# Buffers, tiles and evicting engine in the third stage of a convolution that runs before a recurrent attention loop

## The chip, the cores and the metric

The kernel runs on one core of one Trainium2 chip. The metric is the device time of one execution in microseconds (us). A core has five engines with an in-order instruction stream each: TensorE (PE; its weight loads are shown as PEld), VectorE (DVE), ScalarE (ACT), GpSimd (POOL) and SyncE (SP). DMA transfers are issued from the streams of SP, ACT and POOL, and 16 DMA engines carry them.

## The reference

Two independent parts are computed from separate inputs and laid side by side in the output (2048 rows; 1024 columns each).

Part A is a long convolution with gating:

```
k_shift = sum over t of k_pad[:, t:t+S, :] * shift_k[:, 3-t]     # 4 taps
kv      = k_shift * v
y       = irfft(rfft(kv, 2S) * rfft(ssm_k, 2S))[:S] + kv * ssm_D
a       = q * y
```

Part B is attention with a recurrent memory: the 2048 rows of x are cut into 64 segments of 32 rows, and for each segment in turn

```
h = concat(mem (8 rows), x_s (32 rows))
q, k, v = h @ Wq, h @ Wk, h @ Wv                # 32 heads of 128
o = softmax(mask(q k^T * scale)) v @ Wo
mem, out_s = o[:8], o[8:]
```

## The kernel before

**The order of the work.** `run_a` computes part A (function `a_kernel`), and what part B needs and does not depend on the memory is woven into it: `a_kernel` calls `fill()` once per step of its stages 2 and 3, and `fill` (L663) adds one piece of part B's preparation to the program. After that come the remaining pieces, the V pass, and then the loop over 64 segments, which takes most of the time.

**Part A in three stages.** The transforms are matrix products. Stage 1 (L242) writes the transformed rows of kv and of the kernel to DRAM (`SU1`, `SK1`). Stage 2 (L301 to L398, 17 sets of two halves, so 34 calls of `fill`) reads them back, multiplies and writes `SZ` to DRAM (L318 to L323); its TensorE order is fixed by hand (`tc.manual_schedule`, L384). Stage 3 (L400 to L421) has 16 steps t. Each loads a tile `zt` from `SZ` (L407, 512 KB), runs four matmuls against `G2h` into a PSUM tile `pt` (L410; shown as `y_ps`), and multiplies it with the query on VectorE into `ot` (L417). Every second step loads a query tile `qt` (L414, 512 KB) for two steps and stores an `ot` tile for two steps through POOL (L419, 512 KB). There are four `zt`, two `qt` and two `ot` buffers and three PSUM tiles of two banks.

**The pieces of part B.** `dense` (L617) makes 16 units for one weight group: eight matmuls into a PSUM tile (L623, `kb_ps`), then `evac` (L610) copies it to the `stage` tile. Three groups follow each other, (0,1), (1,0) and (1,1), 48 units. `fill` adds a unit in every call of stage 3 and in two of three calls of stage 2, so that units 22 to 31 end group (1,0) in the last part of stage 2 and in stage 3, units 32 to 38 of group (1,1) lie in stage 3, and nine more come after it (L741). After the 16th unit the group's four stores `RKQ<-stage` are issued from ACT. The last three weight tiles of group (1,1) are loaded by SP (L573 and L577, `pw<-in_B_Wq_dram`, 512 KB each) into places that the last unit of group (1,0) gives free. `x_load` (L588) loads two blocks of x for use by `x_block` (L594): eight transposes into a PSUM tile (L601, `xt_ps`), two VectorE copies into `xt` (L604, L605), one store `REC<-xt` through POOL (L606, 256 KB). Five of the 16 blocks, 11 to 15, fall into stage 3. `kb_ps` and `xt_ps` share two PSUM tiles.

```
def evac(dst, src):
    if units[0] < STAGE3:              # 34: the calls of fill in stage 2
        nc.scalar.copy(dst, src)
    else:
        nc.vector.tensor_copy(dst, src)
```

So ScalarE evicts the units of stage 2 but for the very last one, VectorE those of stage 3, the nine behind it and the V pass. The X tiles and `xt` tiles are the single buffers `wring2` and `wring3`, which the loop's weight ring uses later.

**After stage 3.** SP loads a tile `part` (L869), then the 16 tiles of Wv (L573 and L577; `Wres`, `Wmore`, `pw`), most of them into memory that part A's tiles had. The V pass (L755 to L768) is 32 units of eight matmuls (L764, `vb_ps`), evicted by VectorE and stored by ACT. Then the segment loop begins (L925).

**What sets the order.** Outside the parts ordered by hand, a scheduler places the instructions of each engine, and each engine runs them in that order. A buffer that is used again makes the next writer wait for the last reader. Each transfer signals one of eight completion counters for those issued from SP and ACT together, and one of eight for POOL's, in turn; a transfer waits until the one eight places earlier on its counter has landed. So up to eight transfers from SP and ACT are under way at once, and one instruction that waits in SP's stream holds back all later loads.

Of the kernel before, what the change touches and what calls it, by code (L numbers as in the profile page):

```python
# [9 lines left out]
BF = mybir.dt.bfloat16  # L10
# [23 lines left out]
STAGE3 = 34  # L34
# [18 lines left out]
def a_kernel(ctx: ExitStack, tc, q, k, v, shift_k, ssm_k, ssm_D, outa, ps_sum, slot4, slot16, stage1_done, fill):  # L53
# [19 lines left out]
    def pair_rows(ap2d, t):  # L73
        return ap2d.rearrange("(p r) d -> p (r d)", r=16)[:, 1024 * t:1024 * t + 2048]

    with ExitStack() as c1:
        cw = c1.enter_context(tc.tile_pool(name="a_cw", bufs=1, side="right"))
        io = c1.enter_context(tc.tile_pool(name="a1_io", bufs=2, side="right"))
        wk = c1.enter_context(tc.tile_pool(name="a1_wk", bufs=3, side="right"))
# [221 lines left out]
    with ExitStack() as c2:  # L301
        gio = c2.enter_context(tc.tile_pool(name="a2_io", bufs=3, side="right"))
        wk = c2.enter_context(tc.tile_pool(name="a2_wk", bufs=3, side="right"))
# [95 lines left out]

    with ExitStack() as c3:  # L400
        io = c3.enter_context(tc.tile_pool(name="a3_io", bufs=4, side="right"))
        wk = c3.enter_context(tc.tile_pool(name="a3_wk", bufs=3, side="right"))
        ps_big = c3.enter_context(tc.tile_pool(name="a3_ps", bufs=3, space=PSUM))
        for t in range(16):
            pt = ps_big.tile([128, 1024], F32, tag="big", name="y_ps")
            zt = io.tile([128, 2, 1024], BF, tag="zt", name="zt")
            nc.sync.dma_start(zt[:], SZ.rearrange("m (r h) d -> r m h d", h=2)[t])  # L407
            for hf in range(2):
                for h in range(2):
                    nc.tensor.matmul(pt[:, hf * 512:(hf + 1) * 512], lhsT=G2h[h][:, :],  # L410
                                     rhs=zt[:, h, hf * 512:(hf + 1) * 512], start=(h == 0), stop=(h == 1))
            if t % 2 == 0:
                qt = io.tile([128, 2048], BF, tag="qt", bufs=2, name="qt")
                nc.sync.dma_start(qt[:], pair_rows(q, t))  # L414
                ot = wk.tile([128, 2048], BF, tag="ot", bufs=2, name="ot")
            half = slice(1024 * (t % 2), 1024 * (t % 2) + 1024)
            nc.vector.tensor_tensor(out=ot[:, half], in0=pt[:], in1=qt[:, half], op=ALU.mult)  # L417
            if t % 2:
                nc.gpsimd.dma_start(outa.rearrange("(p r) d -> p r d", r=16)[:, t - 1:t + 1, :],  # L419
                                    ot[:].rearrange("p (r d) -> p r d", r=2))  # L420
            fill()  # L421


def b_kernel(ctx: ExitStack, tc, x, mem0, Wq, Wk, Wv, Wo, outb, n_seg, run_a):
# [28 lines left out]
    def dram_chunk(ch):  # L453
        m, a, g = ch
        return Wo_v[a] if m == 3 else W_v[m][a, g]

    def dst_view(ap, ch):
        return ap.rearrange("p (hh d) -> p hh d", hh=2) if ch[0] == 3 else ap

    def stream_src(ch):  # L460
        return WS[ring_order.index(ch), :, 0:2048]
# [19 lines left out]
    base = ctx.enter_context(tc.tile_pool(name="b0_base", bufs=1, side="right", reuse_waits="tile"))  # L481
# [8 lines left out]
    def pair():  # L490
        turns["pair"] ^= 1
        return base.tile([128, 2048], BF, tag=f"wring{2 + turns['pair']}", name="pair")

    def slot16(shape, dt, name):
        turns["stage"] ^= 1
        return base.tile(shape, dt, tag=f"stage{turns['stage']}", name=name)
# [3 lines left out]
    def pw(k=None):  # L500
        if k is None:
            k = pw_next[0] % 8
            pw_next[0] += 1
        return pring.tile([128, 2048], BF, tag=f"pw{k}", name="pw")
# [80 lines left out]
    copies = []  # L585
    loaded = {}

    def x_load(b):  # L588
        t = base.tile([128, 2048], BF, tag="wring2", name="X_sb")
        x_loads.append(nc.sync.dma_start(t[:].rearrange("p (b d) -> p b d", b=2),  # L590
                                         x[b * 128:(b + 2) * 128, :].rearrange("(b p) d -> p b d", b=2)))
        loaded[b], loaded[b + 1] = t[:, 0:1024], t[:, 1024:2048]

    def x_block(b):  # L594
        X_sb = loaded.pop(b)
        if b % 2 == 0:
            t = base.tile([128, 2048], BF, tag="wring3", name="xt")
            xts[b], xts[b + 1] = t[:, 0:1024], t[:, 1024:2048]
        tp = ps0.tile([128, 1024], BF, tag="ps0", name="xt_ps")
        for kc in range(8):  # L600
            nc.tensor.transpose(tp[:, kc * 128:(kc + 1) * 128], X_sb[:, kc * 128:(kc + 1) * 128], ident[:])  # L601
        xt = xts.pop(b).rearrange("p (s k t) -> p s k t", s=4, k=8)
        rows = tp[:].rearrange("p (k j t) -> p j k t", k=8, j=4)
        nc.vector.tensor_copy(xt[:, :, :, NM:SEG], rows[:, :, :, 0:NX])  # L604
        nc.vector.tensor_copy(xt[:, :, :, 0:NM], rows[:, :, :, NX:SEG])  # L605
        rec_stores.append(nc.gpsimd.dma_start(REC[:, 4 * b:4 * b + 4, :], xt.rearrange("p s k t -> p s (k t)")))  # L606
# [1 line left out]
    xts = {}  # L608
    rec_stores, x_loads = [], []
    def evac(dst, src):  # L610
        if units[0] < STAGE3:
            nc.scalar.copy(dst, src)
        else:
            nc.vector.tensor_copy(dst, src)
# [35 lines left out]
    def store():  # L650
        if stores:
            nc.scalar.dma_start(*stores.pop(0))

    units = [0]
    blocks = list(range(n_seg // 4))
    wo_copies = [ch for ch in ring_order if ch[0] == 3 and ch not in (KEPT_A, KEPT_B)]

    def q1_load(kc, k, ins):
        res[1, kc, 1] = pw(k)[:]
        with tc.issue_after(ins):  # L660
            group(1, 1, which=[kc], ws=q1, held=True)

    def fill(behind=None):  # L663
        store()
        n = units[0]
        units[0] += 1
        if n == 0:
            x_load(0)
        if n >= WO_COPY and wo_copies:
            ch = wo_copies.pop(0)  # L670
            with tc.issue_after(rec_stores[-1].ins):
                nc.gpsimd.dma_start(dst_view(stream_src(ch), ch), dram_chunk(ch))
        if n in Q_LOAD:
            i = Q_LOAD.index(n)
            q1_load(kept_q1[i][1], 4 + i, behind.ins)
        if n > 5 and n % 2 and copies:
            with tc.issue_after(rec_stores[-1].ins):
                copied.append(nc.gpsimd.dma_start(*copies.pop(0)))
        if n % 3 == 2 and blocks:
            b = blocks.pop(0)  # L680
            x_block(b)
            if b % 2 and blocks:
                x_load(b + 1)
        if n >= STAGE3 or n % 3 != 2:
            next(rest, None)

# [6 lines left out]
    def more(i):  # L693
        return wres3.tile([128, 2048], BF, tag=f"Wmore{i}", name="Wmore")
# [43 lines left out]
    with c0p:  # L738
        temps = dict(zip(v_temp, homes_v))
        wv = [group(2, 0, temps), None]  # L740
        for _ in rest:  # L741
            store()
        wv[1] = group(2, 1, temps)
        for i, ch in enumerate(v_temp):
            if i >= 2:
                home = (lambda i=i: more(i)) if i < len(v_temp) - 2 else (lambda k=i - len(v_temp) + 4: pw(k))
                at_hand[ch] = (wv[ch[2]][ch[1]], home)
        while stores:
            store()
        with tc.issue_after(got[-1].ins):  # L750
            for _ in range(2):
                fetch()
        n_k = len(own[0, 0])
        late = late[n_k:-2] + late[4:n_k] + late[:4] + late[-2:]
        for g in range(2):  # L755
            ws = wv[g]
            if g == 0:
                vsts = slot16([128, 4, 4, 512], BF, "vst")
            for tb in range(4):
                vst = vsts[:, tb] if g == 0 else pair()[:].rearrange("p (c w) -> p c w", c=4)  # L760
                for c in range(4):
                    ps = ps0.tile([128, 512], F32, tag="ps0", name="vb_ps")
                    for kc in range(8):
                        v_last = nc.tensor.matmul(ps[:], lhsT=xbt(kc)[:, 16 * tb:16 * tb + 16, :].rearrange("p s t -> p (s t)"),  # L764
                                                  rhs=ws[kc][:, c * 512:(c + 1) * 512], start=(kc == 0), stop=(kc == 7))
                    evac(vst[:, c, :], ps[:])
                nc.scalar.dma_start(
                    VBD[g, 16 * tb:16 * tb + 16].rearrange("s t h e -> (s t) (h e)"), vst.rearrange("p c w -> p (c w)"))  # L768
            if g == 0:
                with tc.issue_after(got[-1].ins):  # L770
                    place_late(4, stage_home)
                    for i in [*range(len(v_temp) - 2, n_more), *range(len(v_temp) - 2)]:
                        place_late(1, lambda: more(i))
                    place_late(1, lambda: pw(2))
                    place_late(4, stage_home)
        assert len(late) == len(at_hand) + 1
# [441 lines left out]
```

## Time and profile before

| | us |
|---|---|
| median of 3 runs | 1750.67 |
| lowest and highest run | 1744.69, 1751.97 |
| the profiled execution | 1745.92 |
| its span in the profile (1.8 lies around it) | 1744.1 |
| last instruction of stage 2's scatter lands; first `zt` load issued | 265.5 |
| last `ot` of stage 3 ends | 329.5 |
| V pass, first PSUM tile complete | 348.2 |
| V pass ends | about 403 |

| engine | busy us | share of the span |
|---|---|---|
| PE | 1645.4 | 94% |
| DVE | 1057.9 | 61% |
| ACT | 665.0 | 38% |
| POOL | 348.9 | 20% |

Times inside the profile are counted from the span's start. A line of the timeline gives start, duration, engine, source line, operation, tile written `<-` tiles read, form and count, and in brackets how long the engine had stood still before it and what released it. An engine name with a q (SPq, ACTq) is its stream issuing a transfer. A line of the stage table gives the stretch, its length, the busy time and the number of instructions of PE, PEld, DVE, ACT and POOL, the TensorE clock granted (1.00 is full), the DMA engines' busy share (it can pass 1 a little) and the GB/s moved. A line of the chain gives start, duration and what the end of the program was waiting for in that piece.

### The profile page before, as it was taken

How to read it: one execution, taken by the hardware profiler on the slowest of the kernel's cores; microseconds unless marked ns; L12 is line 12 of the kernel's file. 1: busy time of each engine (PE TensorE's matmuls, PEld its weight loads, DVE VectorE, ACT ScalarE, POOL GpSimd, SP SyncE). 2: the span in 40 equal slices, each digit the busy share in tenths (PEclk: the TensorE clock that was granted, in tenths of full speed). 3: DMA queues.
4: the chain of work that ended last, by engine and by line, in shares of the span. 5: the costliest groups of instructions: out<-in, count | busy, mean ns of one | idle time of the engine just before them, and what ended most of it. 6: DMA issues, size and time to landing. Idle time of an engine off the chain costs nothing.

```text
span 1744.1 us, 71328 instructions
## 1 busy us (share of the span) xinstructions
PE 1645.4 (94%) x30808; PEld 1007.4 (58%) x30840; DVE 1057.9 (61%) x3480; ACT 665.0 (38%) x1169; POOL 348.9 (20%) x627
## 2 busy tenths in 40 slices
PE   6888886898999999999999999999999999999999
PEld 2443332344666666666666666666666666666665
DVE  9926984434566666555565656665555566666655
ACT  6865760002333333333333333333333333333333
POOL 4102451100111212122111111121221111111211
PEclk9999998999999999999999999999999999999999
DMA  9988988998999999999999999999999999999998
GB/s 335 365 332 304 355 320 320 342 394 320 355 345 363 352 356 353 354 357 360 353 351 346 356 343 356 359 347 349 353 354 345 354 354 359 353 352 353 357 354 293
DMA packets 190208, 607.09 MB, mean 348 GB/s; under 512 B 25714, under 2 KB 34050, under 8 KB 189892
## 3 DMA queue, kind: packets, MB, share of 16 engines
q1 hardware_dynamic: 161092, 534.32, 84.3%
q0 software_dynamic: 20128, 45.13, 7.4%
q10 hardware_dynamic: 8672, 23.07, 3.4%
q8 instruction: 241, 3.95, 0.9%
q14 instruction: 75, 0.61, 0.1%
HBM read 547.37 MB, written 57.67 MB: 347 GB/s over the span
## 4 chain that ended last, share of the span: by engine, by line
PE 70%; DMA 13%; issue 2%; DVE 1%; ACT 0%; SPq 0%; POOL 0%; POOLq 0%; DVEq 0%; ACTq 0%
PE acc L955 37%; PE yacc L1046 23%; DMA wring<-WS 8%; PE vb_ps L764 2%; PE OTp L974 2%; PE OTp L891 2%; PE OTp L1024 1%; DMA out_dram<-ot 1%; DMA pw<-in_B_Wq_dram 1%; PE SB L980 1%; DMA zt<-SZ 1%; DMA Wres<-in_B_Wv_dram 1%; PE kb_ps L623 1%; DMA VBD<-pair 1%; PE SB L983 1%
## 5 line engine op out<-in xcount | busy, mean ns | idle before, releaser
L955 PEld LDWEIGHTS <-rec 128*32 128x32 bf16 x12288 | 305.0, 96 | 293.2 <-DVE rec L902 39.5
L1046 PEld LDWEIGHTS <-OT 128*64 128x64 bf16 x8319 | 430.5, 109 | 50.0 <-ACT E L994 27.1
L965 ACT CAST qkv_sb<-acc 128x512 bf16<-128x512 f32 x320 | 187.6, 586 | 474.5 <-PE acc L955 462.2
L955 PE MATMUL acc<-Wres,rec 128*32 128x512 bf16 x3328 | 253.1, 381 | 1.4 <-issue 0.6
L955 PE MATMUL acc<-wring,rec 128*32 128x512 bf16 x2300 | 230.5, 380 | 7.7 <-DMA wring<-WS 5.0
L955 PE MATMUL acc<-Wmid,rec 128*32 128x512 bf16 x3072 | 224.1, 379 | 3.5 <-issue 3.5
L1046 PE MATMUL yacc<-Wmore,OT 128*64 128x256 bf16 (+1 forms) x2560 | 220.8, 273 | 0.0
L1046 PE MATMUL yacc<-wring,OT 128*64 128x256 bf16 (+1 forms) x2256 | 191.2, 272 | 5.2 <-DMA wring<-WS 3.9
L1077 DVE COPY KT<-OTp 128x512 bf16<-128x512 bf16 x64 | 27.2, 425 | 231.5 <-PE OTp L891 231.5
L1036 ACT CAST OT<-OTp 128x640 bf16<-128x640 f32 x128 | 88.6, 692 | 194.8 <-PE OTp L1028 193.5
L955 PE MATMUL acc<-pw,rec 128*32 128x512 bf16 x1796 | 134.5, 379 | 4.2 <-issue 3.7
L1143 ACT CAST Y<-yacc 128x256 bf16<-128x256 f32 x128 | 47.7, 373 | 231.1 <-PE yacc L1046 231.1
L902 DVE CAST rec<-tps 128x32 bf16<-128x32 f32 x128 | 24.5, 192 | 165.1 <-PE tps L900 165.1
L932 POOL DMA_DIRECT2D VBs<-VBD x128 | 68.4, 534 | 275.2 <-DVE mx L989 60.1
L955 PE MATMUL acc<-Wlate,rec 128*32 128x512 bf16 x1536 | 116.9, 381 | 0.0
L795 DVE TENSOR_SCALAR quarter<-OTp 128x256 int32<-128x256 int32 x252 | 102.2, 420 | 19.6 <-ACT OT L1036 16.9
L1145 POOL DMA_DIRECT2D out_dram<-Y x128 | 65.8, 514 | 219.8 <-ACT Y L1143 216.5
L989 DVE TENSOR_REDUCE mx<-SB 128x8 f32<-128x320 f32 x128 | 63.0, 492 | 67.3 <-PE SB L983 66.0
L886 POOL DMA_DIRECT2D rec_kq<-RKQ x64 | 49.5, 774 | 237.5 <-PE yacc L1046 215.4
L623 PE MATMUL kb_ps<-XBT,pw 128*128 128x512 bf16 x313 | 81.0, 399 | 5.8 <-DVE xt L605 2.6
L881 POOL DMA_DIRECT2D rec<-REC x64 | 35.9, 562 | 237.2 <-PE acc L955 221.2
L1046 PE MATMUL yacc<-Wlate,OT 128*64 128x256 bf16 x1024 | 78.8, 276 | 0.3 <-PE acc L955 0.3
(224 smaller groups left out, 2698.9 us busy)
## 6 DMA issues: line engine op xcount, KB each, us to landing
wring<-WS SPq DMA_DIRECT2D x831, 512.0 KB, 6.1
wring<-WS SPq DMA_DIRECT2D x64, 132.0 KB, 5.0
SK<-s_sb SPq DMA_DIRECT2D x16, 512.0 KB, 4.5
SU<-s_sb SPq DMA_DIRECT2D x16, 512.0 KB, 6.1
Kg<-SK SPq DMA_DIRECT2D x32, 256.0 KB, 5.5
Ug<-SU SPq DMA_DIRECT2D x32, 256.0 KB, 5.4
RKQ<-stage ACTq DMA_DIRECT2D x16, 512.0 KB, 8.0
zt<-SZ SPq DMA_DIRECT2D x16, 512.0 KB, 8.3
```

The costliest lines, as they stand in the source:

```text
L623: nc.tensor.matmul(ps[:], lhsT=ws[kc][:, hl * 128:(hl + 1) * 128], rhs=xbt(kc).rearrange("p s t -> p (s t)"), start=(kc == 0), stop=(kc == 7))
L795: nc.vector.tensor_scalar(out=dst, in0=src, scalar1=0, scalar2=None, op0=ALU.bitwise_or)
L881: nc.gpsimd.dma_start(rec[:], REC[:, s, :])
L886: nc.gpsimd.dma_start(rec[:].rearrange("p (j c) -> p j c", j=4), RKQ[s // 16, :, :, s % 16, :].rearrange("j p c -> p j c"))
L932: nc.gpsimd.dma_start(VB[:, 0:128], VBD[g, s].rearrange("t h e -> h t e"))
L955: nc.tensor.matmul(self.acc[32 * c:32 * c + 32, :], lhsT=hT[:, ch[1], :], rhs=w[:, 512 * c:512 * c + 512], start=(ch == chs[0]), stop=(ch ...
L965: nc.scalar.copy(sb, self.acc[:])
L989: nc.vector.tensor_reduce(out=mx[:], in_=S, op=ALU.max, axis=AX.X)
L1036: nc.scalar.copy(OT[:], o_view)
L1046: nc.tensor.matmul(yacc[f][64 * dh:64 * dh + m, x - o:y - o], lhsT=lhsT, rhs=r, start=(h == (0, 2 * FIRST[-1])[f] and x == o), stop=stop, ...
L1143: nc.scalar.copy(Y[:, 256 * f:256 * f + 256], yacc[f][:, 0:256])
L1145: nc.gpsimd.dma_start(bass.AP(outb.tensor, outb.offset + SEG * s * 2048 + 512 * dh, [[2048, 32], [1, 512]]), Y[64 * dh + NM:64 * dh + 40, :])
```

## The change

Three groups of edits, all for stage 3 and the pieces of part B woven into it:

1. `ot` has four buffers in place of two, `zt` six in place of four, `qt` three in place of two.
2. In stage 3 the x blocks get tiles of their own (`X_sb` and `xt`, two buffers each, pool `a3_x`) in place of `wring2` and `wring3`. Block 11 still uses the X tile that stage 2 loaded.
3. `evac` uses ScalarE until a flag is set at the start of the V pass. So 26 evictions move from VectorE to ScalarE: the last unit of stage 2, 16 in stage 3 and nine behind it. The V pass stays on VectorE.

```
-        wk = c3.enter_context(tc.tile_pool(name="a3_wk", bufs=3, side="right"))
+        wk = c3.enter_context(tc.tile_pool(name="a3_wk", bufs=4, side="right"))
         ps_big = c3.enter_context(tc.tile_pool(name="a3_ps", bufs=3, space=PSUM))
+        xp = c3.enter_context(tc.tile_pool(name="a3_x", bufs=2, side="right"))
         for t in range(16):
             pt = ps_big.tile([128, 1024], F32, tag="big", name="y_ps")
-            zt = io.tile([128, 2, 1024], BF, tag="zt", name="zt")
+            zt = io.tile([128, 2, 1024], BF, tag="zt", bufs=6, name="zt")
...
-                qt = io.tile([128, 2048], BF, tag="qt", bufs=2, name="qt")
+                qt = io.tile([128, 2048], BF, tag="qt", bufs=3, name="qt")
...
-                ot = wk.tile([128, 2048], BF, tag="ot", bufs=2, name="ot")
+                ot = wk.tile([128, 2048], BF, tag="ot", name="ot")
...
-            fill()
+            fill(pool=xp)
...
-    def x_load(b):
-        t = base.tile([128, 2048], BF, tag="wring2", name="X_sb")
+    def x_load(b, pool=None):
+        t = pool.tile([128, 2048], BF, tag="X_sb", name="X_sb") if pool else base.tile([128, 2048], BF, tag="wring2", name="X_sb")
...
-    def x_block(b):
+    def x_block(b, pool=None):
...
-            t = base.tile([128, 2048], BF, tag="wring3", name="xt")
+            t = pool.tile([128, 2048], BF, tag="xt", name="xt") if pool else base.tile([128, 2048], BF, tag="wring3", name="xt")
...
-        if units[0] < STAGE3:
+        if not v_pass[0]:
             nc.scalar.copy(dst, src)
...
-    units = [0]
+    units, v_pass = [0], [False]
...
-    def fill(behind=None):
+    def fill(behind=None, pool=None):
...
-            x_block(b)
+            x_block(b, pool)
             if b % 2 and blocks:
-                x_load(b + 1)
+                x_load(b + 1, pool)
...
         late = late[n_k:-2] + late[4:n_k] + late[:4] + late[-2:]
+        v_pass[0] = True
```

In the programs as built, TensorE has the same instructions before and after, in another order in stage 3; the scheduler also places the loads of stage 3 otherwise in SP's stream. Before, two `qt` loads and the X load for blocks 12 and 13 stand ahead of the first `zt` load; after, they stand behind the first or second `zt` load (order: zt, qt, zt, X, zt, qt, zt, zt, qt, zt). In stage 2 only the order of the last two matmuls of its last unit against two of `kb_ps` differs. No tile has another address but X, `xt`, `zt`, `qt` and `ot` of stage 3.

## The prediction

> **What bounds the kernel now.** I read the page's 40 slices first: PE is at 9 tenths in every slice from the eleventh on, and the built programs are the same there, addresses too. So only the part before the loop can change, and the loop starts when the V pass ends. The V pass is dense on PE (L764 in the chain, about 56 us), so the question is when it starts. Next came the stage table, in 10 us steps, from stage 3's first loads to the V pass:
>
> ```profile
> 260.00:270.00 10.00, 7.67 (x44) 3.64 (x45) 3.52 (x6) 0.59 (x1) 0.57 (x1) 1.00 0.84 277
> 270.00:280.00 10.00, 9.43 (x45) 4.25 (x44) 5.88 (x7) 0.00 (x0) 2.02 (x3) 1.00 0.88 297
> 280.00:290.00 10.00, 5.26 (x25) 2.65 (x24) 5.38 (x7) 0.00 (x0) 0.73 (x1) 0.83 0.79 308
> 290.00:300.00 10.00, 4.83 (x27) 2.12 (x26) 4.55 (x7) 0.00 (x0) 1.85 (x3) 0.93 1.02 359
> 300.00:310.00 10.00, 4.75 (x11) 1.58 (x12) 1.22 (x1) 0.00 (x0) 1.30 (x3) 0.50 1.03 419
> 310.00:320.00 10.00, 9.13 (x39) 3.75 (x38) 4.53 (x5) 0.00 (x0) 1.26 (x2) 0.88 1.03 419
> 320.00:330.00 10.00, 8.61 (x45) 4.01 (x44) 7.73 (x12) 0.00 (x0) 1.35 (x3) 1.00 0.70 246
> ```
>
> The first column after the length is PE: it stands still some 20 us between 260 and 330. But the last two columns (DMA share, GB/s) are full from 290 to 320. PE's timeline names its waits:
>
> ```profile
> 269.63 1.04 PE L410 MATMUL y_ps<-zt,G2h 128*128 128x512 bf16 x3 [2.33 <-DMA zt<-SZ]
> ...
> 285.42 0.48 PE L601 MATMUL xt_ps<-ident,X_sb 128*128 128x128 bf16 x3 [4.52 <-DVE stage L614]
> ...
> 298.51 0.48 PE L623 MATMUL kb_ps<-XBT,pw 128*128 128x512 bf16 x1 [2.60 <-DVE xt L605]
> 303.81 1.87 PE L410 MATMUL y_ps<-zt,G2h 128*128 128x512 bf16 x4 [4.82 <-DMA zt<-SZ]
> 306.90 1.89 PE L623 MATMUL kb_ps<-XBT,pw 128*128 128x512 bf16 x4 [1.23 <-DMA pw<-in_B_Wq_dram]
> ...
> 327.12 1.02 PE L410 MATMUL y_ps<-zt,G2h 128*128 128x512 bf16 x4 [0.41 <-DMA zt<-SZ]
> 327.98 17.43 PE L623 MATMUL kb_ps<-XBT,pw 128*128 128x512 bf16 x78
> ```
>
> Two kinds of wait: evictions that VectorE makes late (4.52, 2.60), and loads. The first kind is one chain: VectorE's own timeline shows it standing behind a store, and everything behind that instruction, the `kb_ps` eviction too, stands with it:
>
> ```profile
> 283.54 1.22 DVE L417 TENSOR_TENSOR ot<-y_ps,qt 128x1024 bf16<-128x1024 f32 x1 [6.80 <-DMA out_dram<-ot]
> ```
>
> Last, the chain of waits: between stage 3 and the V pass it is made of loads.
>
> ```profile
> 294.48 14.86 DMA pw<-in_B_Wq_dram
> ...
> 337.04 10.68 DMA Wres<-in_B_Wv_dram
> 347.77 8.79 PE vb_ps L764 x40
> ```
>
> **What the edits take away, add and move.** Four `ot` buffers take away the 6.80 us behind the store (and 1.73 us at 326.58). ScalarE's evictions take 26 copies of 0.69 us from VectorE, at 0.59 us each (L612) on an engine with no copy between 262 and 345; together these end PE's 4.52. Own `xt` tiles end the 2.60 (VectorE's L604 waited 3.17 us for `REC<-xt`). PE thus gains up to 7 us where nothing else ends last. ScalarE's stream has the four `RKQ` stores between the evictions; they wait for loads that landed long before, so I cost them at nothing.
>
> What is late next is the loads, in three steps.
>
> *Step 1, the end of stage 3's loads.* I count in 512 KB transfers. Full stretches (290 to 320) move 359, 419 and 419 GB/s, mean 399: 524,288 B take 1.31 us; the ends are 1.25 (419) and 1.46 (359). From the first `zt` (PE takes it at 269.6) to the sixteenth (327.1), 39 are carried: 25 from SP (15 `zt`, 6 `qt`, 1 X, 3 `pw`), 4 `RKQ`, 2 `WS`, 6 `out_dram`, 4 `REC` of half size. 39 x 1.31 = 51.1 of 57.5 us, so 6.4 us of transfer time are lost, mostly where SP's stream waits for a buffer (L414 for VectorE 5.9, L407 for PE 2.5). With more buffers the first ten loads wait for nothing but landings, so I recover these 6.4. But the change also moves three transfers into this stretch: two `qt` and the X load are issued at 255.05 to 261.69 now, and will stand behind the first `zt` load, which waits for `SZ<-zs` to land at 265.5. That adds 3 x 1.31 = 3.9. 42 x 1.31 = 55.0: the last `zt` at 324.6, **2.5 us earlier**. The ends: 322.1 (1.25) and 330.9 (1.46).
>
> *Step 2, group (1,1)'s weights.* They wait for unit 31 on PE, so I follow PE through its new order: five units end at 267.3; y0 at 269.6, y1 at 272.2 (its load is third), the X transposes at 273.5, then a `zt` every 2 to 3 us with a unit (eight matmuls, 1.73 us) between, the seventh at about 285.5; 0.87 for its four matmuls and ten of 0.216: 288.6 (now 292.3, SP's issue at L573). The third of the loads must now wait until the first has landed (same counter, eight places on); before, the first took 7.1 us (292.27, releasing L407 at 299.40). Counted like step 1, with 29.5 transfers up to it (20 SP, 4 `RKQ`, 4 `out_dram`, 1.5 `REC`): 269.6 + 28.5 x 1.31 = 306.9, against 294.48 + 14.86 = 309.3 now: **2.4 earlier**. From there PE now needs 345.2 - 309.3 = 35.9 us to the V pass, 2.1 of it waits for `zt`: 340.7 to 342.8.
>
> *Step 3, which path ends last.* From the last `zt`: 324.6 + 0.87 (y15) + 80 matmuls (17.26 from 327.98 to 345.24) = 342.7. So this or step 2's upper end, the same within 0.1. Wv: now the last `ot` ends at 329.5 and the eighth tile lands at 347.7, 18.2 later, with some 1.9 of it a wait of SP for the last output store (until 334.94), which in the program after stands behind the eighth tile. The last `ot` then ends near 326.8; 16.3 to 18.2 on: 343.1 to 345.0. The first V group needs it 1.5 us into the pass, at 344.2, so I take no wait (0.85 now). The group is complete at 342.7 + 1.7 = 344.4 against 348.2.
>
> **The sum**: 3.8 us. It passes through the V pass and the loop whole, since the loads behind the V pass wait for PE there (SP stands 13.7 us at L727 for `vb_ps`) and move with it. On the profiled execution: 1745.9 - 3.8 = 1742. That one lies at the low end of what was shown (1744.69, 1745.92, 1750.67, 1751.97; mean 1748.3), so for a median I forecast 1748.3 - 3.8, rounded to **1744**; its own range, with steps 1 and 2 at nearby rates and the runs' scatter, is 1741 to 1748.
>
> **Rivals** (times at the mean 1748.3).
>
> *PE becomes the bound.* If the transfers go at 1.25 us and the last three stores yield to loads, the last `zt` lands at 318.4 and `pw` at 305.3. PE then reaches y15 at 305.3 + 17.8 - 2.1 = 321.0, the V pass at 339.1, 6.1 earlier, its first group 7.4; and if the idle spell before is too short for the clock to fall (0.50 in 300 to 310; ten matmuls took 3.98 in place of 2.2, four y matmuls 1.87 in place of 1.03), 2.6 more. So 7 to 10 earlier: 1740. For it: the 419 of two whole stretches. Against: even so PE waits for `pw` some 10 us. Chance 0.26.
>
> *Nothing.* The idle DMA time is only recovered as far as the three moved transfers use it up: 1748. Chance 0.10.
>
> *A wait takes the place of the one removed (slower).* The third `pw` load stands in SP's stream until the first lands, and nine loads of stage 3 behind it. If that landing takes not 7.1 but 13.5 us, as the loads issued at 293 and 294 did, the third is issued at 302 and lands some 8.5 transfers later, at 313.2; the V pass starts at 313.2 + 35.9 = 349.1, 3.9 later; with 14.86, 5.2 later: 1753. It decides from a landing of 9.7 us on, where `pw` comes at 309.3 as now. Against: at 288.6 only about three loads are ahead of it. Chance 0.09.
>
> *The transfers are slower.* If the mix goes at the 359 GB/s of 290 to 300 all along, the last `zt` comes at 330.9, the V pass at 349.0, its first group 2.6 later than now: 1751. Against: the two stretches at 419. Chance 0.05. The Trainium skill, "DMA: Bandwidth & Descriptors", section "Where 436 GB/s comes from", speaks for this one: it holds that for transfers between HBM and SBUF the limit per core is about 358 GB/s, so that more buffers could not raise the rate of a full stretch; by that rule 42 transfers take 61.5 us, and the change is slower by about 3. The trace disagrees with it at 300 to 320, where the core moved 419 GB/s. The same page, section "Queues, rings and completion order", says that each DMA engine serves the queues that have work in turn; the latencies of 13 to 15 us here, with loads, `RKQ` and output stores under way together, agree.
>
> **Chances.** The forecast's case has 0.50. A difference of 0.5% (8.7 us) is about what a measurement of this kernel can tell from no change. Faster by more: the upper part of the PE case, 0.18, and the forecast's tail by scatter, 0.07: 0.25. Slower by more: only the wait's case with scatter on top: 0.08. Within: 0.67. The range reaches from the PE case (1748.3 - 10, and a little scatter: 1737) to the wait's (1753).
>
> **What would show it.** Right: no wait of PE for DVE in stage 3; VectorE's `ot` never behind `out_dram`; DMA share at 1 from 268 to about 325; PE standing some 10 us before group (1,1) for `pw`; last y near 325; first V group near 344. Step 1 is wrong if the share still has gaps below 0.9 before 320; step 2 if the third `pw` load is issued after 298. The forecast fails if the loop's step length moves, since I take it as unchanged.

## The result and the profile after

| | before | after |
|---|---|---|
| median of 10 runs, us | 1746.06 | 1741.57 |
| lowest to highest | 1744.69 to 1751.97 | 1736.15 to 1748.08 |
| the profiled execution | 1745.92 | 1741.86 |
| its span | 1744.1 | 1740.1 |

The ratio is 0.9966, 95% interval 0.9951 to 0.9982: 5.9 us less, between 3.1 and 8.6. The medians differ by 4.5, the two profiled executions by 4.06.

The stage table after, in the same 10 us steps (busy time and instructions of PE, PEld, DVE, ACT, POOL; granted clock, DMA share, GB/s):

```profile
260.00:270.00 10.00, 8.70 (x44) 3.73 (x43) 1.38 (x3) 3.03 (x6) 0.91 (x2) 1.00 0.73 234
270.00:280.00 10.00, 8.36 (x44) 3.89 (x44) 5.72 (x7) 1.17 (x2) 1.33 (x3) 1.00 1.02 385
280.00:290.00 10.00, 8.36 (x42) 3.54 (x41) 4.80 (x6) 1.28 (x3) 1.97 (x3) 1.00 1.03 419
290.00:300.00 10.00, 2.29 (x15) 1.04 (x14) 2.66 (x4) 0.48 (x1) 1.29 (x2) 0.80 1.03 417
300.00:310.00 10.00, 7.25 (x23) 2.42 (x22) 1.22 (x1) 0.59 (x1) 1.80 (x3) 0.69 1.02 416
310.00:320.00 10.00, 7.71 (x42) 3.42 (x41) 4.47 (x4) 1.76 (x3) 0.74 (x1) 1.00 1.03 420
320.00:330.00 10.00, 10.00 (x48) 4.52 (x47) 3.98 (x7) 2.73 (x5) 2.57 (x4) 1.00 0.61 211
```

The DMA engines are full from 270 to 320 now, where they stood at 0.79 to 0.88 from 270 to 290 before. PE does more from 280 to 290 (8.36 in place of 5.26) and then stands longer. PE's timeline says for what:

```profile
268.75 1.02 PE L411 MATMUL y_ps<-zt,G2h 128*128 128x512 bf16 x4 [0.84 <-DMA zt<-SZ]
...
299.64 1.86 PE L411 MATMUL y_ps<-zt,G2h 128*128 128x512 bf16 x4 [6.18 <-DMA zt<-SZ]
302.90 3.74 PE L624 MATMUL kb_ps<-XBT,pw 128*128 128x512 bf16 x9 [1.40 <-DMA pw<-in_B_Wq_dram]
...
315.15 1.04 PE L411 MATMUL y_ps<-zt,G2h 128*128 128x512 bf16 x4 [0.81 <-DMA zt<-SZ]
...
323.38 1.03 PE L411 MATMUL y_ps<-zt,G2h 128*128 128x512 bf16 x4
324.24 17.43 PE L624 MATMUL kb_ps<-XBT,pw 128*128 128x512 bf16 x80
341.50 1.03 PE L766 MATMUL vb_ps<-Wres,XBT 128*128 128x512 bf16 x4
...
344.41 1.24 PE L766 MATMUL vb_ps<-Wres,XBT 128*128 128x512 bf16 x5 [0.87 <-DMA Wres<-in_B_Wv_dram]
```

The waits for `stage` (4.52) and for `xt` (2.60) are gone, but for remains of 0.46 us at most; one wait for a load has grown from 4.82 to 6.18, and the clock still falls in it: four y matmuls take 1.86 in place of 1.02. The last four y matmuls (323.38) no longer wait for their load. VectorE's waits from 262 to 330 (total us, times, longest) are none for a store any more:

```profile
DVE ot L418 <- PE y_ps L411: 25.1, 12, 7.3
DVE ot L418 <- DMA qt<-in_A_q_dram: 14.0, 4, 7.6
DVE xt L605 <- PE xt_ps L602: 2.7, 3, 1.7
```

And the chain of waits runs through loads and one store until 315.15. From there PE is what ends last, up to the last `ot` of stage 3 at 324.44, and then the Wv loads that are issued behind it:

```profile
274.07 14.29 DMA zt<-SZ
...
290.88 12.15 DMA RKQ<-stage
...
303.05 0.33 SPq L408
...
303.42 11.68 DMA zt<-SZ
...
331.23 13.14 DMA Wres<-in_B_Wv_dram
344.41 40.10 PE vb_ps L766 x185
```

The `RKQ` store in it is a counter: the `zt` load issued at 303.05 is on the counter of a store issued at 290.88 and had to wait until that had landed; the load behind it in SP's stream, the thirteenth, went out at 303.42, and it is the last `zt` load that PE waits for (at 315.15).

**The measure used below.** Whole executions scatter by some 5 us, in code that no edit touches: in the profiles taken here the last `z_ps` matmul of stage 2 starts between 258.2 and 262.0, and the loop takes 1329 to 1341 us whatever the kernel. So I compare the stretch from that last `z_ps` to the first `vb_ps` matmul of the V pass. Before, and after:

```profile
260.72 0.39 PE L376 MATMUL z_ps<-Yim,Nim 64*128 64x512 bf16 x1
...
345.24 1.03 PE L764 MATMUL vb_ps<-Wres,XBT 128*128 128x512 bf16 x4
```

```profile
260.98 0.38 PE L376 MATMUL z_ps<-Yim,Nim 64*128 64x512 bf16 x1
...
341.50 1.03 PE L766 MATMUL vb_ps<-Wres,XBT 128*128 128x512 bf16 x4
```

That is 84.52 and 80.52 us. The table has all kernels; "loop" is the time from the same `z_ps` to the first `acc` matmul of the loop, and a ratio is against runs of the kernel before on the same chip.

| kernel | stretch | loop | last y matmuls start, from `z_ps` | ratio (95%) |
|---|---|---|---|---|
| before, first and second profile | 84.5, 84.8 | 143.6, 143.3 | 66.4, 66.6 | |
| after, first and second profile | 80.5, 80.4 | 140.0, 138.7 | 62.4, 62.2 | 0.9966 (0.9951 to 0.9982) |
| buffers alone | 79.4 | 139.6 | 61.3 | 0.9971 (0.9947 to 0.9995) |
| own x tiles alone, twice | 78.0, 81.3 | 138.2, 142.0 | 59.9, 63.2 | 0.9988 (0.9968 to 1.0008), 0.9989 (0.9973 to 1.0006) |
| ScalarE's evictions alone | 81.4 | 140.9 | 63.7 | 0.9977 (0.9952 to 1.0002) |
| all but ScalarE's evictions | 79.6 | 139.1 | 61.5 | 0.9973 (0.9950 to 0.9995) |
| five `qt` loads left out | 78.0 | 134.8 | 59.8 | |
| `qt` loads early | 78.5 | 137.8 | 60.4 | |
| stores held | 75.5 | 136.0 | 57.4 | |
| units first | 78.1 | 141.1 | 64.1 | |
| `qt` loads early and stores held | 74.0 | 135.0 | 55.9 | 0.9954 (0.9934 to 0.9973) |

### The profile page after: what moved, and what is told of

The parts are those of the page before. It is cut to its first block, busy times and chain, and to the rows that moved or that the text cites. A ratio compares the mean times of both kernels' runs of the same rounds, so it can differ in the third digit from the quotient of the medians.

```text
span 1740.1 us, 71348 instructions
## 1 busy us (share of the span) xinstructions
PE 1647.2 (95%) x30840; PEld 1003.3 (58%) x30840; DVE 1040.8 (60%) x3454; ACT 679.9 (39%) x1195; POOL 350.3 (20%) x627
## 4 chain that ended last, share of the span: by engine, by line
PE 76%; DMA 15%; DVE 4%; issue 2%; ACT 2%; SPq 0%; POOL 0%; DVEq 0%; POOLq 0%; ACTq 0%
PE acc L957 37%; PE yacc L1048 22%; DMA wring<-WS 10%; PE kb_ps L624 4%; PE vb_ps L766 3%; PE OTp L976 2%; DMA zt<-SZ 2%; PE OTp L893 2%; ACT s_sb L249 1%; PE OTp L1026 1%; DMA RKQ<-stage 1%; PE SB L982 1%; PE s_ps L247 1%; DMA Wres<-in_B_Wv_dram 1%; PE ks_ps L285 1%
```

## The experiments

**Is the measure sharp enough?** Both kernels were profiled a second time, unchanged.

> The kernel before, unchanged, for a second profile. The stretch from the last `z_ps` matmul of stage 2 to the first `vb_ps` matmul was 84.5 us in its first profile, 80.5 with the whole change, and 79.4, 78.0 and 81.4 with one group of edits alone. Theory (transfers lost to waits for buffers are what the change recovers): 83 to 86 again, with a gap in the DMA engines' share between the first and last `zt`. Rival (scatter): the first profile was an unlucky one; 82 or less, and the difference between the kernels is inside the scatter.

> The changed kernel, unchanged, for a second profile: the stretch from the last `z_ps` to the first `vb_ps` was 80.5 us. Theory: 79.5 to 81.5 again, since full DMA engines leave little room for chance. Rival (scatter): more than 2 us away from 80.5, so that single profiles don't tell the parts apart.

84.76 beside 84.52, and 80.38 beside 80.52: the difference of 4.2 us between the kernels is not scatter. VectorE's 6.80 behind the store (6.84 the second time) and PE's 4.52 (4.17) come back in the second profile of before. Not every kernel repeats so well: see the own x tiles below.

**Each part alone.** The three groups of edits, one at a time on the kernel before, and the change without the third. The third alone is

```
-        if units[0] < STAGE3:
+        if not v_pass[0]:
             nc.scalar.copy(dst, src)
```

with the flag; the others are the lines of their group in the diff above. The scheduler places SP's loads otherwise in each of these programs (with buffers alone the X load and one `zt` load stand ahead of the first `qt` load, with own x tiles alone two `zt` loads stand ahead of the X load, behind the two `qt` loads; with ScalarE's evictions alone the order is close to that of before). So a part is its edit together with that order.

> The kernel before with the first group of edits alone: four `ot`, six `zt`, three `qt` buffers. Theory (transfers): the change gains because stage 3's loads no longer wait for buffers, so that the DMA engines lose no time between the first and the last `zt`; what PE waits for besides is mostly filled by the next late load. Then the V pass starts at 342 to 343.5 (before 345.2, after the whole change 341.5), and the kernel is 2 to 3 us faster than before. Rival (evictions): what made PE late was VectorE, standing behind stores with `kb_ps` evictions queued behind it; the `xt` tile is still single here and VectorE still evicts, so at least the wait for `xt` (2.60) stays and less than 2 us is gained: V pass at 344 or later.

> The kernel before with the second group of edits alone: own X and `xt` tiles in stage 3, two buffers each. Theory (transfers): PE's wait of 2.60 us for `xt` goes, but PE then waits that much longer for the next load, since `ot` still holds up SP's stream: V pass within 1 us of 345.2, time within 1 us of before. Rival (evictions): the 2.60 us are gained whole: V pass at about 342.6.

> The kernel before with the third group of edits alone: 26 evictions on ScalarE in place of VectorE. Theory (transfers): PE's waits for an eviction behind a standing VectorE go, but the two `ot` buffers still hold up VectorE and SP's loads, so PE waits for `zt` in their place: V pass within 1.5 us of 345.2. Rival (evictions): most of the 3.7 us by which the V pass moved comes from here: V pass at 342.5 or earlier.

> The changed kernel with VectorE evicting the 26 tiles as before (the first two groups of edits alone). Theory (transfers): with four `ot` buffers VectorE no longer stands, and each of its copies costs PE nothing: V pass within 0.8 us of 341.5, time within 1 us of the changed kernel's, 3 to 4.5 us below before. Rival (evictions): VectorE's `ot` multiplications, which wait for `qt` loads, still hold up evictions queued behind them; at least half of the gain goes: V pass at 343.5 or later.

The V pass started at 338.48, 336.90, 341.79 and 338.69; since the last `z_ps` differs from run to run, the stretches 79.4, 78.0, 81.4 and 79.6 are what to compare. Neither theory came out. The transfer theory gave the x tiles and ScalarE's evictions next to nothing, and each alone takes off 3 us or more; the eviction theory gave the buffers less than 2 us, and they take off 5. Every part alone gives three quarters of the whole's 4.2 us or more, and together they would give 11 us or more if they added up; 3 us of a single one is of the size by which two profiles of one program differ (see the last run below), 11 against 4.2 is not. Without ScalarE's evictions the stretch is 79.6, as the transfer theory had it. (The timed ratios are too wide to rank them: 0.9971, 0.9988 and 0.9977 alone, 0.9966 together, all intervals overlapping.) So the three are not three gains that add up: they cut the same chain in three places. In the kernel before that chain is closed: VectorE waits for an output store, `kb_ps` and `xt_ps` evictions stand behind it, so PE is late with the transposes, and SP's stream stands on the X load until they are done, with all loads behind it. Here are SP's own lines of before:

```profile
277.19 0.65 SPq L407 DMA_DIRECT2D zt<-SZ  x1
288.16 0.38 SPq L590 DMA_DIRECT2D X_sb<-in_B_x_dram  x1
```

and the sum of its waits from 250 to 346:

```profile
SPq L590 <- PE xt_ps L601: 15.8, 2, 10.3
...
SPq L414 <- DVE ot L417: 5.9, 2, 4.1
```

10.3 us without a load: this is the gap in the DMA share at 280 to 290. With `ot` buffers VectorE does not stand, and SP's wait at that X load falls to 4.0 us; with own X tiles the X load does not wait for PE at all (SP's waits for VectorE at the `qt` loads stay, 14.3 us in four pieces of at most 4.8); with ScalarE's evictions the X load waits 5.3 us, VectorE stands even longer, and PE waits for it only 2.1 us, for `xt`. The DMA share from 280 to 290 is 1.03, 1.02 and 1.01 with one part alone, in place of 0.79. VectorE's lines with ScalarE's evictions alone:

```profile
284.17 2.35 DVE L417 TENSOR_TENSOR ot<-y_ps,qt 128x1024 bf16<-128x1024 f32 x2 [7.11 <-DMA out_dram<-ot]
296.88 1.22 DVE L417 TENSOR_TENSOR ot<-y_ps,qt 128x1024 bf16<-128x1024 f32 x1 [7.42 <-DMA out_dram<-ot]
```

14.5 us behind stores, against 8.5 before, and yet a stretch 3 us shorter: a wait of an engine costs only what is queued behind it.

**What binds now: DMA bandwidth?** Five of the eight `qt` loads left out:

```
-                qt = io.tile([128, 2048], BF, tag="qt", bufs=3, name="qt")
-                nc.sync.dma_start(qt[:], pair_rows(q, t))
+                if t < 6:
+                    qt = io.tile([128, 2048], BF, tag="qt", bufs=3, name="qt")
+                    nc.sync.dma_start(qt[:], pair_rows(q, t))
```

> The changed kernel with five of the eight `qt` loads left out: the steps from the sixth on multiply with the third tile loaded, so part A's output is another. Five transfers of 1.25 us less between the first and the last `zt`, nothing else. Theory (transfers): stage 3 is bound by the DMA engines, so the stretch from the last `z_ps` to the first `vb_ps` shrinks by 4 to 6.3 us, to 74.2 to 76.5. Rival (TensorE or evictions bind it): it stays within 1 us of 80.5. Rival (eight counters: SP's loads wait for the landing eight places earlier, whatever the bandwidth): five places less per counter, so the loads come earlier, but by the latency of a landing less, and DMA engines show gaps between 275 and 315.

The stretch is 78.0, 2.5 us less: short of the 4 that the transfer theory asked for at least, and too much for its rivals. PE's timeline shows why:

```profile
299.00 6.26 PE L625 MATMUL kb_ps<-XBT,pw 128*128 128x512 bf16 x15 [5.34 <-DMA pw<-in_B_Wq_dram]
...
309.20 1.02 PE L411 MATMUL y_ps<-zt,G2h 128*128 128x512 bf16 x4 [2.03 <-DMA zt<-SZ]
...
311.71 1.02 PE L411 MATMUL y_ps<-zt,G2h 128*128 128x512 bf16 x4 [0.62 <-DMA zt<-SZ]
...
319.92 1.03 PE L411 MATMUL y_ps<-zt,G2h 128*128 128x512 bf16 x4
```

and the chain of waits:

```profile
288.94 10.19 DMA RKQ<-stage
...
299.14 12.52 DMA zt<-SZ
...
311.71 1.02 PE y_ps L411 x4
```

The fifteenth `zt` load lands at 314.48, 2.9 us before PE gets to it (317.33), and PE does not wait for the sixteenth either. What PE waits for last is the thirteenth, at 311.71; from there it has 26.34 us of work to the V pass without a wait. In the changed kernel the last wait is for the same load, at 315.15, and the V pass follows 26.35 us later. Counted from the last `z_ps` that load came after 51.6 us in place of 54.2, and this is the whole gain. Only three of the five left-out loads stood ahead of it in SP's stream, so at most 3 x 1.25 = 3.8 us could come off; my expectation had counted all five. In both kernels it is held by the counter of an `RKQ` store (issued here at 288.94, landed at 299.13), so part of the rival with the eight counters is true; the gaps that it forecast are not there (DMA share 1.00 or more in every 5 us from 270 to 310). In the changed kernel, then, the end is neither the third `pw` load, after whose landing at 305.34 PE still stood 3.6 us for `zt` loads, nor the last `zt` load, which landed 0.6 us before PE got to it (322.81 and 323.38), but a load between them.

**And if `pw` comes early?** The units dealt out otherwise over the 16 steps:

```
+PER = [3, 3, 3, 1] + [0] * 5 + [1] * 6 + [0]
...
-        if n >= STAGE3 or n % 3 != 2:
-            next(rest, None)
+        if n >= STAGE3:
+            for _ in range(PER[n - STAGE3]):
+                next(rest, None)
+        elif n % 3 != 2:
+            next(rest, None)
```

> The changed kernel with the dense units of stage 3 dealt out otherwise over its 16 steps: three each in the first three steps, one in the fourth, none in the next five, one in the next six, none in the last, so that unit 31 is done after four or five steps in place of nine, and the last three loads of group (1,1) stand in SP's stream behind the sixth `zt` load in place of the ninth. The number of transfers is the same. Theory A (the third `pw` load sets the start): it is issued some 5 us earlier and lands 7 to 8 us earlier, so that path allows 73 to 75; the path over the last `zt` load (61.4 to 61.8 behind the last `z_ps`, as now, then a step and 61 matmuls of 0.216) allows 76; the stretch is 76 to 77.5. Theory B (the last `zt` load set it): no less than 80, since that load comes no earlier and fewer units stand behind it only where PE has done them meanwhile; 79.5 to 80.5. Rival (units in front hold back the steps, so the `zt` buffers come free late and the DMA engines stand): a gap in the DMA share between 270 and 285, stretch 80 to 83.

```profile
287.79 1.69 PE L627 MATMUL kb_ps<-XBT,pw 128*128 128x512 bf16 x7 [1.38 <-DMA pw<-in_B_Wq_dram]
...
299.57 1.86 PE L411 MATMUL y_ps<-zt,G2h 128*128 128x512 bf16 x4 [6.99 <-DMA zt<-SZ]
302.67 1.03 PE L605 MATMUL xt_ps<-ident,X_sb 128*128 128x128 bf16 x8 [1.24 <-DMA X_sb<-in_B_x_dram]
...
323.19 1.03 PE L411 MATMUL y_ps<-zt,G2h 128*128 128x512 bf16 x4
324.06 13.33 PE L627 MATMUL kb_ps<-XBT,pw 128*128 128x512 bf16 x61
```

Now the third `pw` load lands 28.6 us after the last `z_ps` (287.75), in place of 44.4, and PE waits 6.99 us for a `zt` load instead and last for the X load, which is on the counter of an `RKQ` store as well. The stretch is 78.1, because 61 matmuls stand behind the last step in place of 80 (4.1 us less) and that step comes later: theory A named this path and put it at 76 to 77.5, because it took the last step as no later than in the changed kernel (62.4 and 62.2 from `z_ps`), and it came at 64.1. The shorter stretch did not last either: the V pass waited for Wv, which is issued behind stage 3 as before, and the loop starts 1 to 2 us later than in the changed kernel. With the run before this one: early `pw` loads alone do not free PE. In both runs the last load that it waits for on the way to the V pass is another (a `zt` load, the X load), and both stood behind an `RKQ` store. That reading rests on what PE waits for in each run; the gain of some 2.5 us in each is of the size by which single profiles can differ.

**What shortens every path: less in front.** The four `RKQ` stores of group (1,0) are issued at 290.51 to 292.19 in the changed kernel, ahead of the last six `zt` loads. ScalarE's stream now issues them later, the first at 315.06:

```
+HOLD = 48
...
-            nc.scalar.copy(dst, src)
+            evacs.append(nc.scalar.copy(dst, src))
...
     def store():
-        if stores:
+        if units[0] < 34 and stores:
             nc.scalar.dma_start(*stores.pop(0))
+        if units[0] >= HOLD and stores:
+            with tc.issue_after(evacs[-1].ins):
+                nc.scalar.dma_start(*stores.pop(0))
```

> The changed kernel with the four `RKQ` stores of group (1,0) held back in ScalarE's stream: they follow the evictions of units 36 to 39, behind the last `zt` load, in place of standing beside the loads of group (1,1)'s last weights. Nothing else is moved. Theory A (the last weight of group (1,1) sets the start of the V pass: in each kernel so far the third `pw` load landed 35 to 36 us ahead of it): that load shares the DMA engines with the four stores now; without them it lands 3.3 to 4 transfers of 1.25 us earlier, and the stretch from the last `z_ps` to the first `vb_ps` falls from 80.4 to 75.5 to 77. Theory B (the last `zt` load sets it, 17.3 us and one step ahead): four transfers leave that path as well, but PE's waits in front of the last steps only change their name; 75 to 76, with the last `zt` landing at 318 and PE waiting for it. Rival (the stores are hidden: what ends last is PE and the eviction): 79.5 to 80.5.

75.5: 4.9 us less, four transfers. Counted from the last `z_ps`, the second `pw` load came after 39.6 us (299.53) in place of 41.9, and the last `zt` after 57.1 (317.10) in place of 61.8. Theories A and B both fit in size, and this run does not tell them apart; what PE waits for last is the load of neither, but the fourteenth `zt` (1.47 us, at 312.14). The rival that the stores are hidden is out. Nor does it tell the stores' transfer time (4 x 1.25 = 5.0 us; the last `zt` came 4.7 earlier) from their counters: the eleventh `zt` load now goes out 29.3 us after the last `z_ps` in place of 38.8, since no store is on its counter. Part of the gain is given back behind:

```profile
335.52 1.03 PE L772 MATMUL vb_ps<-Wres,XBT 128*128 128x512 bf16 x4
336.38 0.38 PE L772 MATMUL vb_ps<-Wmore,XBT 128*128 128x512 bf16 x1
337.45 0.38 PE L772 MATMUL vb_ps<-Wres,XBT 128*128 128x512 bf16 x1 [0.69 <-DMA Wres<-in_B_Wv_dram]
338.73 0.38 PE L772 MATMUL vb_ps<-Wres,XBT 128*128 128x512 bf16 x1 [0.90 <-DMA Wres<-in_B_Wv_dram]
340.01 1.24 PE L772 MATMUL vb_ps<-Wres,XBT 128*128 128x512 bf16 x5 [0.90 <-DMA Wres<-in_B_Wv_dram]
```

2.5 us of waits in the first V group, where the held stores and the Wv loads meet; at the start of the loop 2.7 to 4.0 us are left (136.0 against 138.7 and 140.0).

**The other transfers in front.** The pools in another order put the `qt` and X tiles where stage 2's buffers come free first, so three `qt` loads stand ahead of the first `zt` load. Addresses, and TensorE's order of some steps against units, change with it.

```
+        qp = c3.enter_context(tc.tile_pool(name="a3_q", bufs=3, side="right"))
+        xp = c3.enter_context(tc.tile_pool(name="a3_x", bufs=2, side="right"))
         io = c3.enter_context(tc.tile_pool(name="a3_io", bufs=4, side="right"))
...
-        xp = c3.enter_context(tc.tile_pool(name="a3_x", bufs=2, side="right"))
...
-                qt = io.tile([128, 2048], BF, tag="qt", bufs=3, name="qt")
+                qt = qp.tile([128, 2048], BF, tag="qt", name="qt")
```

> The changed kernel with the pools of stage 3 opened in another order (the three `qt` tiles and the x tiles first, then `zt`), so that three `qt` loads stand ahead of the first `zt` load in SP's stream, as two did before the change. Theory (transfers): three transfers leave the full stretch, 3.75 to 3.9 us; the last `SZ` store lands up to 1.2 us later, as in the kernel before: the stretch from the last `z_ps` to the first `vb_ps` is 77 to 78.5 us. Rival (the store's delay counts whole, since what comes between is bound elsewhere): 80.5 to 81.7.

78.5, at the edge of the 77 to 78.5 of the theory and 2 us below the changed kernel; the first `zt` load was issued 5.8 us after the last `z_ps` in place of 3.3 to 3.5. The sum has the right sign and size, but the own x tiles below scattered by 3.3, so this run alone does not prove it.

**Both moves.**

> The two moves that helped, together: the changed kernel with the three `qt` loads ahead of the first `zt` load and the four `RKQ` stores held back to units 36 to 39. From the last `z_ps`: first `vb_ps` after 78.5 us with the first move alone, 75.5 with the second (80.4 and 80.5 for the change as it was), first matmul of the loop after 137.8 and 136.0 (140.0 and 138.7). Theory (transfers ahead of the third `pw` load): the moves take different transfers out of its way and add up, less what the Wv loads behind the last `ot` don't follow: first `vb_ps` at 73 to 75, loop at 134 to 136, time 4 us below the changed kernel's, 8 to 9 below before. Rival (Wv binds now): held stores and Wv loads meet, PE waits for `Wres` in the first group, and the loop starts no earlier than with the stores held alone, 135.7 to 136.5.

The stretch is 74.0 and the loop starts at 135.0, as the theory had it, though 2.0 us of waits for `Wres` are there too. Against early `qt` loads alone (78.5) held stores take off 4.5 us, so that their 4.9 has come out a second time. Against before the time is 0.9954 (0.9934 to 0.9973), 8.0 us less, at medians of 1739.16 and 1747.39. It beats the kernel before. That it also beats the change as it was shows in the profiles (6.5 us in the stretch, 3.7 to 5.0 at the loop), but the intervals of the times overlap.

**A run that tested something else.** The last kernel was to hold the stores back with own x tiles alone.

> The kernel before with own X and `xt` tiles (the second group of edits alone) and the four `RKQ` stores held back until VectorE has evicted units 36 to 39; buffers and evicting engine as before. Theory (the transfers ahead of the third `pw` load, not buffers or engines, set the start of the V pass): first `vb_ps` 3.5 to 4.8 us earlier than with own tiles alone (78.0), at 73.2 to 74.5, as good as with the whole change and both moves. Rival (with two `ot` and four `zt` buffers SP's loads wait again as soon as the stores are out of the way): 76 to 78.

The order that this asked for was already that of the kernel's streams: ScalarE has no evictions there to stand behind, an order between two engines added no wait, and the built program was, instruction for instruction, that of the own x tiles alone. The stores went out at 290.35. So its question stays open, and the run is a second one of the same program: 81.3 in place of 78.0. Differences of up to some 3 us between single profiles are therefore not to be read by themselves; the 4.2 us of the change (two profiles each), the 4.9 and the 6.5 us of the held stores are beyond that.

## Why the prediction was right, point by point

- **The size.** 3.8 us were forecast for the point where the first V group is complete. From the last `z_ps` it starts its ninth matmul at 83.7 and 82.4 after, at 87.3 and 86.9 before: 4.0 on the mean. The loop starts 4.0 earlier as well, and the loop's own length shows no difference beyond its scatter (1335.5 and 1337.2 before, 1334.7 and 1338.2 after). That the sum came so close is partly luck: it was made of 2.5 us for the start of the V pass and 1.3 for waits for Wv inside the first group that would go. The start moved by 4.2, and from it to the ninth matmul nothing was gained (2.7 and 2.1 before, 3.1 and 2.0 after). The median came out at 1741.57 in place of 1744; 2.2 of these 2.4 us are the base, taken as 1748.3 from four runs where ten gave 1746.06.
- **Step 1, the last `zt`**: 324.6 forecast, 322.81 measured. The span it covers was right (42 transfers in 54.1 us, 55.0 forecast); its start was not. The first `zt` load goes out 3.46 and 3.34 us after the last `z_ps`, in place of 4.79 both times: the `SZ` store ahead of it landed in 2.35 and 2.22 us in place of 3.74 both times. I had counted what the three moved loads cost later and had left the store as it was; that is 1.4 us. That the loads were what slowed the store is not shown: both `qt` loads had landed (260.45, 261.70) when it was issued at 261.76, only the X load went out beside it, and the one program of own x tiles alone gave 1.99 and 3.36 in its two profiles. And I put the lost transfer time down to L414 (5.9) and L407 (2.5), where the longest wait of SP's stream was the X load's 10.3 at L590, in the same view. The sum did not need the name; the edit that removes it did.
- **Step 2, `pw`**: issued at 287.21 (288.6 forecast), landed after 6.22 (7.1), the third issued at 293.50 because it waits for that, as forecast, and landed at 305.34 (306.9). From there to the V pass 36.2 (35.9), of which PE stood 3.6 for `zt` loads (2.1).
- **Step 3, which path ends last**: "this or step 2's upper end, the same within 0.1". Neither did: PE's last wait on the way to the V pass was for the thirteenth `zt` load at 315.15 (316.00 in the second profile), held by the counter of an `RKQ` store. The last `zt` was 0.6 us short of it, so the sum lost little by that; `pw` was further off, since PE stood 3.6 us for `zt` loads after it. The V pass started at 341.50 in place of 342.7, and I took no wait for `Wres`; there were 1.07 us in the first profile and none in the second.
- **The edits' cost and cover.** ScalarE's evictions at nothing, and the `RKQ` stores among them: no wait of theirs is on the chain but as a counter (12.15). As transfers, which the count of step 1 has, they turned out to be worth more: 4.9 us when they were moved. Without ScalarE's evictions the stretch is the same within scatter (79.6). That together the edits "end PE's 4.52" was right, but any one of them would have done it; the text did not ask that. That own `xt` tiles end the 2.60 was wrong: with own x tiles alone VectorE no longer waits for `REC`, yet PE still waits 2.6 us for `xt`, whose second copy stands behind an `ot` on VectorE; with buffers alone and the single `xt` it waits 1.1.
- **PE as the bound** (rival): no. PE stood 6.18 and 1.40 us for loads, and the clock fell to 0.69, so neither the 7 us nor the 2.6 came.
- **Nothing** (rival): no, the two profiles of each exclude it.
- **A wait in place of the one removed** (rival): the wait is there, 3.2 us of SP for the first `pw` load to land, but that took 6.22 us and not 9.7.
- **Slow transfers** (rival): no, 416 to 420 GB/s from 280 to 320.

## What to carry to other kernels

Look first at the queue of the engine that issues the loads, and at its longest wait in a stretch in which the transfer engines are not full: here that was 10.3 us on one X load, at a share of 0.79. A long wait of that queue alone says little: in the changed kernel SP stood 8.9 us for PE at the first `pw` load, and the engines stayed full. When several waits form one chain, cutting it once brings most of the gain, and the next cuts little. With the engines full, the other edits added nothing to the buffers here (79.4 alone, 80.5 and 80.4 together); then ask which transfers stand in front of the load that PE waits for last and need not, as the four stores here (4.9 us for a move of four instructions). Before shortening a path, find that load in the trace: it was neither of the two that I had followed.

## What the runs showed of the hardware

- The fullest 10 us of stage 3 moved 417 to 421 GB/s in every kernel here, 1.25 us for 512 KB: no change of buffers, order or engine moved that figure.
- The last `SZ` store ahead of the dependent `zt` load landed in 2.35 and 2.22 us in the two profiles of the kernel after and in 3.74 in both of before, but in 1.99 and 3.36 in two profiles of one program (own x tiles alone): a single such time can't be put down to an edit.
- After PE had stood 4.8 to 7.0 us for a load, four matmuls took 1.86 or 1.87 us in place of 1.02: before, after, with the stores held and with the units first alike. The length of the wait alone does not decide it: behind a wait of 1.56 us near 271, four matmuls took 1.86 with the stores held and with five `qt` loads left out, and 1.02 in the changed kernel.
